# The weight-ring refills of experts with five slots or more, each issued one slot later

## The chip, the cores and the metric

The kernel runs on one core of one Trainium2 chip. The metric is the device time of one execution in microseconds (us), the median of the runs; lower is better. Engines are named as the profile names them: PE is TensorE (matmul), PEld its weight load, DVE is VectorE, ACT is ScalarE, POOL is GpSimd, SP is SyncE. SP does no arithmetic here. It issues the transfers (DMAs) one behind the other, each after the semaphore waits that it carries.

## What is computed

Attention over chunks of 64 keys, a feed-forward layer with a leaky activation, and a mixture of eight experts in which each token goes to the one expert with the largest gate value. The part that the change touches is the last:

```python
logits = x @ w_gate                       # x: 4608 tokens of 512
expert_idx = np.argmax(logits, axis=1)    # 8 experts
...
for e in range(E):
    xe = x[expert_idx == e]
    h = np.maximum(xe @ w1[e], 0.0)       # 512 -> 1024
    ye = h @ w2[e]                        # 1024 -> 512
    out[expert_idx == e] = gate_w[expert_idx == e, None] * ye
```

The reference, computed on the given inputs, sends 384, 175, 1053, 582, 1271, 128, 556 and 459 tokens to experts 0 to 7, that is 3, 2, 9, 5, 10, 1, 5 and 4 tiles of 128 tokens.

## The kernel before

The first 930 us or so hold attention, the feed-forward layer and the gate. Meanwhile the expert weights are split into two float32r parts each and written to a DRAM scratch, `wsp`, four pieces of 2 MB for each expert (two of `w1`, two of `w2`). The rest, some 440 us, runs the experts.

**Slots.** The expert part is cut into slots. A slot is one tile of up to 128 tokens of one expert. `TS` = 39 slots are unrolled in the program, and which expert a slot has is known on the chip alone: table code on DVE (the functions `table_...`) works it out from the token counts, and the slots read it from the tile `rt`. The expert with most tokens comes first, the second largest next, then the others by number, and the one with fewest slots last. With the counts above: expert 4 has slots 0 to 9, expert 2 has 10 to 18, expert 0 has 19 to 21, expert 1 has 22 and 23, expert 3 has 24 to 28, expert 6 has 29 to 33, expert 7 has 34 to 37, expert 5 has 38.

**A slot's work on PE.** `m1(t, 0)` and `m1(t, 1)` multiply the tokens by the two pieces of `w1`, `m2(t, 0)` and `m2(t, 1)` by the two pieces of `w2`, 12 matmuls each. The order on PE in the loop is m1(t+1, 0), m1(t+1, 1), m2(t, 0), m2(t, 1). All lie on line 680.

**The weight ring.** Four buffers in SBUF, `ring[0]` to `ring[3]`, hold pieces 0 and 1 of `w1` and 0 and 1 of `w2` (as buffers 2 and 3), and each has two halves: while one expert is computed from one half, the next expert's weights are loaded into the other. `refill(t, c)`, line 870, is the transfer that loads buffer c for the next expert. It is issued in every slot from 4 on, but carries a condition that SP reads from `rt` (line 866): only where the condition is 1 do its 2 MB move. In this text (t, c) is the refill of buffer c that is issued for slot t, and one whose condition is 1 is said to be sent.

**The order on SP.** The pass of the loop for slot t issues refill(t, 0), refill(t, 1), refill(t-1, 2), refill(t-1, 3), and then `load(t+4)`: four transfers of token rows (`xg`, line 648) and one of gate values (`gi`, line 651). That is nine transfers in a pass. They take turns on eight completion semaphores, and a transfer is issued once the one eight places before it is complete; a refill whose condition is 0 is complete at once. So gi waits for the first refill of its own pass, and the first, second and third refill of a pass for the second, third and fourth of the pass before. In the order list each refill also waits for the last matmuls of slot t-1 that read its buffer.

**What PE waits for.** Slots read their ring half by a register, so the program cannot tell which half a refill writes. Matmuls of slots t and t+1 are declared free of refill (t, c); those of slot t+2 on buffer c wait for it, whether it loads their half or the other one, and for a refill that is not sent that wait is nothing.

**The conditions.** `table_refill` (lines 843 to 863) writes the conditions, in rows 3 to 6 of `rt`. `mt` is the expert's number of slots less 2, `rr` the slot's place in its expert from 0, `far` is 1 for an expert of five slots or more. Only experts between the first and the last have refills (`has`).

Of the kernel before, what the change touches and what calls it, by code (L numbers as in the profile page):

```python
# [12 lines left out]
ALU = mybir.AluOpType  # L13
# [29 lines left out]
def tile_attention_moe(ctx, tc, q, k, v, w_in, w_out, alpha, w_gate, w1, w2, out):  # L43
# [15 lines left out]
    T = NTILE + 2 * (E - 1)  # L59
# [525 lines left out]
    V = nc.vector  # L585
# [134 lines left out]
    def tbl(shape, name, dt=F32):  # L720
        tb[name] = P2["tb"].tile(shape, dt, name=name)
        return tb[name]

    def bc(x, a, b, p=128):
        return x.unsqueeze(1).to_broadcast([p, b - a, E])
# [90 lines left out]
    def slot_sum(dst, vals):  # L816
        w = tb["w"][o1]
        V.tensor_tensor(out=w, in0=tb["oh"][o1], in1=vals, op=ALU.mult)
        V.tensor_reduce(out=dst, in_=w, axis=AX.X, op=ALU.add)
# [23 lines left out]
    def table_refill():  # L843
        q_ = tb["ordt"]
        mt, rr, cm, has = (tbl([1, T], x) for x in ("mt", "rr", "cm", "has"))
        mo = tbl([1, 1], "mo")
        V.tensor_reduce(out=mo, in_=tb["pos8"][o1, 1], axis=AX.X, op=ALU.max)
        V.tensor_scalar(out=has, in0=q_, scalar1=mo[:, 0:1], scalar2=None, op0=ALU.is_lt)
        V.scalar_tensor_tensor(out=has, in0=q_, scalar=0.5, in1=has, op0=ALU.is_gt, op1=ALU.mult)
        V.scalar_tensor_tensor(out=has, in0=tio[o1], scalar=tb["S"][o1, 0:1], in1=has, op0=ALU.is_lt, op1=ALU.mult)  # L850
        slot_sum(mt, bc(tb["m"][o1], 0, T, 1))
        slot_sum(rr, tb["d"][o1])
        V.tensor_copy(out=rt[:, 7, T:T + 1], in_=tb["S"][o1])
        V.tensor_scalar(out=mt, in0=mt, scalar1=-2.0, scalar2=None, op0=ALU.add)
        far = tbl([1, T], "far")
        V.tensor_scalar(out=far, in0=mt, scalar1=3.0, scalar2=None, op0=ALU.is_ge)
        for c in range(4):
            if c in (1, 2):
                V.scalar_tensor_tensor(out=cm, in0=mt, scalar=float(c - 1), in1=far, op0=ALU.min, op1=ALU.add)
                V.tensor_tensor(out=cm, in0=cm, in1=rr, op=ALU.is_equal)  # L860
            else:
                V.scalar_tensor_tensor(out=cm, in0=mt, scalar=float(c), in1=rr, op0=ALU.min, op1=ALU.is_equal)
            V.tensor_tensor(out=rt[:, 3 + c, 0:T], in0=cm, in1=has, op=ALU.mult)

    def refill(t, c):
# [23 lines left out]
    for t in range(3):  # L889
# [12 lines left out]
        (tx, 4), (m1, 3, 0), (table_order,), (m2, 1, 0), (m1, 3, 1), (m2, 1, 1), (load, 5), (m2, 2, 0), (th, 3, 0),  # L902
        (tx, 5), (m2, 2, 1), (table_next,), (load, 6), (th, 3, 1), (m1, 4, 0), (m1, 4, 1), (tx, 6), (th, 4, 0),
        (table_base, 8, T), (m2, 3, 0), (th, 4, 1), (load, 7), (m1, 5, 0), (table_refill,), (refill, 4, 0),
        (m2, 3, 1), (th, 5, 0), (m1, 5, 1), (refill, 4, 1), (load, 8), (m2, 4, 0), (th, 5, 1), (m2, 4, 1),
    )
# [125 lines left out]
```

## Time and profile before

| | |
|---|---|
| runs, median of 3 | 1383.49 us (1378.62 to 1383.83) |
| the profiled execution | 1386.75 us |
| its span, first to last instruction | 1385.0 us |
| PE busy | 1327.6 us, 96% of the span |
| DVE, ACT, POOL busy | 1029.0, 818.4, 745.7 us |

The profile is of one execution, 3.3 us above the median. Its span is read as a sequence of stages with different limits. PE is busy nearly throughout, so what counts is where it is not, and what ended those gaps. The timeline of SP shows four refills (`ring<-wsp`) in a line "x4", then four `xg` and one `gi`; it shows all refills, sent or not. The start of an issue that had to wait is the end of that wait.

### The profile page before, as it was taken

Reading aid. Unit: us, or ns where it says so; the run is one execution under the profiler, and the core shown is the slowest. Engines: PE = TensorE matmul, PEld = TensorE weight load, DVE = VectorE, ACT = ScalarE, POOL = GpSimd, SP = SyncE. Lnnn points to the kernel's source line nnn. Section 1 sums busy time; section 2 is a strip of 40 time slices with the busy share of each in tenths; the row PEclk is TensorE's granted clock in tenths of the full one; section 3 lists DMA queues with packets and bytes.
Section 4 is the critical chain, followed back from the end, with each engine's and each line's share of the span. In section 5 each row is a group of like instructions: output and inputs, shape, how many; then the busy total and the mean of one; then the engine's idle time right before and its main releaser. Section 6 shows DMA issues by size and latency. Waiting matters only on the chain. (4 is left out here: it accounts for less than half of the span.)

```text
span 1385.0 us, 31135 instructions
## 1 busy us (share of the span) xinstructions
PE 1327.6 (96%) x9515; PEld 1155.2 (83%) x9515; DVE 1029.0 (74%) x2529; ACT 818.4 (59%) x2281; POOL 745.7 (54%) x754
## 2 busy tenths in 40 slices
PE   7788999999999999999999999999999999989997
PEld 6667888999999999999989999887788888868885
DVE  7996688888788778878887886568975666546653
ACT  4554565666656565565656565439566656655663
POOL 4554456666666666666575764333444444434443
PEclk9999999999999999999999999999999999999999
DMA  6546445556556655665566561194124525866572
GB/s 233 197 151 179 145 170 191 184 190 206 200 182 191 197 190 186 206 198 168 197 200 200 182 206 39 41 370 176 47 55 157 181 66 204 331 206 229 177 273 94
DMA packets 107306, 249.16 MB, mean 180 GB/s; under 512 B 15552, under 2 KB 36544, under 8 KB 103040
## 3 DMA queue, kind: packets, MB, share of 16 engines
q1 hardware_dynamic: 101136, 227.37, 49.7%
q0 software_dynamic: 6000, 19.70, 3.7%
q8 instruction: 84, 1.38, 0.4%
q14 instruction: 86, 0.70, 0.2%
HBM read 401.39 MB, written 88.91 MB: 354 GB/s over the span
## 5 line engine op out<-in xcount | busy, mean ns | idle before, releaser
L330 PEld LDWEIGHTS h<-xt,ring 128*128 128x128 f32 x3456 | 457.0, 193 | 41.8 <-DVE xt L317 4.0
L330 PE MATMUL h<-xt,ring 128*128 128x256 f32 x3456 | 466.8, 285 | 14.3 <-DVE xt L317 3.5
L382 PE MATMUL y<-ring,g 128*128 128x512 f32 x1728 | 457.4, 400 | 5.1 <-POOL g L360 3.8
L382 PEld LDWEIGHTS y<-ring,g 128*128 128x128 f32 x1728 | 307.5, 190 | 62.7 <-POOL g L360 6.0
L360 POOL TENSOR_TENSOR g<-r,g 128x256 fp32r<-128x256 f32 x281 | 250.4, 894 | 136.9 <-ACT g L356 121.1
L406 DVE CUSTOM_DVE_ANT_0 junk<-row,wgb 128x512 bf16<-128x512 f32 x288 | 268.0, 930 | 7.8 <-ACT row L394 3.6
L470 POOL TENSOR_TENSOR sp<-eraw,sp 128x512 fp32r<-128x512 f32 x128 | 181.8, 1421 | 132.1 <-ACT sp L469 116.6
L698 DVE TENSOR_SCALAR hx<-h 32x128 f32<-32x128 f32 x576 | 165.3, 287 | 96.8 <-PE h L680 89.3
L680 PE MATMUL h<-ring,xT 128*128 (+1 forms) x936 | 221.8, 393 | 6.4 <-DMA ring<-wsp 4.4
L680 PE MATMUL y<-ring,hT 128*128 (+1 forms) x936 | 221.0, 390 | 5.8 <-POOL hT L668 3.1
L668 POOL TENSOR_TENSOR hT<-z,hT 128x512 fp32r<-128x512 f32 x78 | 101.1, 1315 | 227.6 <-ACT hT L667 227.6
L680 PEld LDWEIGHTS h<-ring,xT 128*128 128x128 f32 x936 | 177.2, 190 | 44.5 <-issue 7.0
L680 PEld LDWEIGHTS y<-ring,hT 128*128 128x128 f32 x936 | 174.9, 188 | 45.6 <-POOL hT L668 5.6
L356 ACT ACTIVATE g<-r 128x256 fp32r<-128x256 f32 x288 | 119.4, 415 | 152.0 <-DVE r L352 109.9
L346 ACT ACTIVATE r<-h 128x256 f32<-128x256 f32 x288 | 110.1, 382 | 159.3 <-POOL g L360 76.0
L696 ACT ACTIVATE hx<-h 32x128 f32<-32x128 f32 x672 | 180.3, 268 | 17.4 <-PE h L680 9.9
L667 ACT ACTIVATE hT<-z 128x512 fp32r<-128x512 f32 x78 | 48.0, 633 | 115.6 <-DVE z L665 111.3
L259 ACT ACTIVATE px<-s 32x256 f32<-32x256 f32 x240 | 89.8, 374 | 3.8 <-DVE s L248 0.9
L469 ACT ACTIVATE sp<-eraw 128x512 fp32r<-128x512 f32 x128 | 81.1, 633 | 1.0
L665 DVE STREAM_TRANSPOSE z<-xg 128x512 f32<-128x512 f32 x39 | 27.5, 706 | 47.6 <-POOL hT L668 47.6
L668 POOL TENSOR_TENSOR xT<-z,xT 128x512 fp32r<-128x512 f32 x39 | 52.1, 1336 | 16.8 <-ACT xT L667 16.3
L271 POOL TENSOR_TENSOR px<-px,sr 128x512 f32<-128x512 f32 x30 | 34.1, 1136 | 39.9 <-DVE sr L270 39.9
(737 smaller groups left out, 1193.3 us busy)
## 6 DMA issues: line engine op xcount, KB each, us to landing
ring<-wsp SPq DMA_DIRECT2D x148, 2048.0 KB
wsp<-sp SPq DMA_DIRECT2D x128, 512.0 KB
eraw<-in_w SPq DMA_DIRECT2D x128, 256.0 KB
xg<-xs SPq DMA_DIRECT2D x156, 64.0 KB
vt<-in_v SPq DMA_DIRECT2D x18, 512.0 KB
qt<-in_q SPq DMA_DIRECT2D x17, 512.0 KB
kt<-in_k SPq DMA_DIRECT2D x17, 512.0 KB
iraw<-in_w_in SPq DMA_DIRECT2D x16, 512.0 KB
```

What stands on the lines that cost most here:

```text
L259: nc.scalar.activation(out=p[J:J + 32, t], in_=s[I:I + 32, e], func=ACTF.Exp, scale=scale)
L330: nc.tensor.matmul(out=h, lhsT=w[:, wl, a, 128 * mi:128 * mi + 128], rhs=x[:, xl, a], start=(n == 0), stop=(n == 11),)
L346: nc.scalar.activation(out=r, in_=h, func=ACTF.Relu)
L356: nc.scalar.activation(out=gs[j, m][:, 0], in_=rs[j, m][0], func=ACTF.Copy)
L360: eng.tensor_tensor(out=g[:, 1], in0=r, in1=g[:, 0].bitcast(F32), op=ALU.subtract)
L382: nc.tensor.matmul(out=ys[j][t], lhsT=g[:, gl, 128 * t:128 * t + 128], rhs=w[:, wl, mi], start=(m == 0 and n == 0), stop=(m == MF - 1 and ...
L406: nc.vector.tensor_tensor_reduce(out=junk, in0=r[:, 0:512], in1=wgb[e // 2][:, e % 2], scale=1.0, scalar=0.0, op0=ALU.mult, op1=ALU.add, a ...
L470: eng.tensor_tensor(out=dst[:, 1], in0=raw, in1=dst[:, 0].bitcast(F32), op=ALU.subtract)
L668: nc.gpsimd.tensor_tensor(out=dst[:, 1], in0=z, in1=dst[:, 0].bitcast(F32), op=ALU.subtract)
L680: ins.append(nc.tensor.matmul(out=out, lhsT=lhs[:, xl, a], rhs=w[:, rows_, wl, a], start=(first and a == 0 and n == 0), stop=(last and a = ...
L696: nc.scalar.activation(out=dst, in_=src, func=ACTF.Relu)
L698: V.tensor_scalar(out=dst, in0=src, scalar1=0.0, scalar2=None, op0=ALU.max)
```

## The change

For experts of five slots or more, three of the four refills go out one slot later: buffer 0 in the second slot (before: the first), buffer 1 in the third (before: the second), buffer 2 in the fourth (before: the third). Buffer 3 stays in the fourth. For experts with fewer slots nothing changes. With the slots above the refills are sent for these slots:

| expert (slots) | buffers 0, 1, 2, 3 before | buffers 0, 1, 2, 3 now |
|---|---|---|
| 2 (10 to 18) | 10, 11, 12, 13 | 11, 12, 13, 13 |
| 0 (19 to 21) | 19, 19, 20, 20 | the same |
| 1 (22, 23) | 22, 22, 22, 22 | the same |
| 3 (24 to 28) | 24, 25, 26, 27 | 25, 26, 27, 27 |
| 6 (29 to 33) | 29, 30, 31, 32 | 30, 31, 32, 32 |
| 7 (34 to 37) | 34, 34, 35, 36 | the same |

```diff
         far = tbl([1, T], "far")
+        far2 = tbl([1, T], "far2")
         V.tensor_scalar(out=far, in0=mt, scalar1=3.0, scalar2=None, op0=ALU.is_ge)
+        V.tensor_scalar(out=far2, in0=far, scalar1=2.0, scalar2=None, op0=ALU.mult)
         for c in range(4):
-            if c in (1, 2):
-                V.scalar_tensor_tensor(out=cm, in0=mt, scalar=float(c - 1), in1=far, op0=ALU.min, op1=ALU.add)
+            if c == 0:
+                V.tensor_tensor(out=cm, in0=far, in1=rr, op=ALU.is_equal)
+            elif c < 3:
+                V.scalar_tensor_tensor(out=cm, in0=mt, scalar=float(c - 1), in1=far2, op0=ALU.min, op1=ALU.add)
                 V.tensor_tensor(out=cm, in0=cm, in1=rr, op=ALU.is_equal)
             else:
-                V.scalar_tensor_tensor(out=cm, in0=mt, scalar=float(c), in1=rr, op0=ALU.min, op1=ALU.is_equal)
+                V.scalar_tensor_tensor(out=cm, in0=mt, scalar=3.0, in1=rr, op0=ALU.min, op1=ALU.is_equal)
             V.tensor_tensor(out=rt[:, 3 + c, 0:T], in0=cm, in1=has, op=ALU.mult)
```

No instruction changes its place on PE, ACT, POOL or SP: the refills stand where they stood, and only the value that each condition has at run time differs. On DVE, in the table code between slots 4 and 5, these rows stand in another form (`cm` holds one buffer's comparison, `mt`, `rr`, `has` and `far` are as above; far_13743 is `far2`):

```order
-L856 TENSOR_SCALAR far<-mt 1x50
-L862 SCALAR_TENSOR_TENSOR cm<-mt,rr 1x50
...
-L859 SCALAR_TENSOR_TENSOR cm<-mt,far 1x50
...
+L857 TENSOR_SCALAR far<-mt 1x50
+L858 TENSOR_SCALAR far_13743<-far 1x50
+L861 TENSOR_TENSOR cm<-far,rr 1x50
...
+L863 SCALAR_TENSOR_TENSOR cm<-mt,far_13743 1x50
```

One row is added (L858), one takes another operation (L862 becomes L861), and the rows for buffers 1 and 2 read `far2` in place of `far`; nothing else on DVE moves.

## Rows read from the trace of the kernel before

**Rows 1.** The page's first line.

```profile
span 1385.0 us, 31135 instructions
```

**Rows 2.** Waits of PE, 1001 to 1366: total us, times, longest us.

```profile
PE h L680 <- DMA ring<-wsp: 4.4, 1, 4.4
PE h L680 <- DVE cm L860: 1.6, 1, 1.6
PE y L680 <- DMA ring<-wsp: 0.4, 1, 0.4
```

**Rows 3.** Timeline of PE, 1214 to 1240: start us, us, instruction, idle time before.

```profile
1217.61 2.99 PE L680 MATMUL y<-ring,hT 128*128 x12 [0.41 <-DMA ring<-wsp]
1225.01 8.17 PE L680 MATMUL h<-ring,xT 128*128 x24 [4.41 <-DMA ring<-wsp]
1233.01 5.60 PE L680 MATMUL y<-ring,hT 128*128 x24
```

**Rows 4.** Busy time, PE clock (PEclk) and DMA of three stretches, by windows.

```profile
1220.40:1225.00 4.60, 0.20 (x1) 0.02 (x1) 0.96 (x2) 2.23 (x4) 3.86 (x4) 0.83 0.59 179
1225.00:1231.00 6.00, 5.99 (x16) 4.71 (x17) 0.00 (x0) 0.45 (x2) 0.93 (x1) 0.56 0.33 88
...
1001.00:1006.00 5.00, 4.42 (x20) 3.72 (x21) 4.67 (x17) 0.83 (x2) 2.30 (x2) 1.00 0.30 93
```

**Rows 5.** The same view, 1204 to 1223; the last two columns: DMA share, GB/s.

```profile
1204.00:1223.00 19.00, 16.19 (x71) 12.82 (x69) 12.88 (x37) 10.86 (x32) 7.21 (x7) 1.00 1.01 373
```

**Rows 6.** Waits of SP's queue, 1001.5 to 1340: total us, times, longest us.

```profile
SPq L870 <- DMA ring<-wsp: 22.7, 10, 4.6
SPq L651 <- DMA ring<-wsp: 12.8, 6, 3.3
...
SPq L870 <- PE y L680: 0.2, 1, 0.2
```

**Rows 7.** Timeline of SP, 1195 to 1260 (start us, us from first to last issue).

```profile
1200.29 4.87 SPq L870 DMA_DIRECT2D ring<-wsp  x4
...
1210.72 8.11 SPq L870 DMA_DIRECT2D ring<-wsp  x4
...
1225.01 0.35 SPq L651 DMA_DIRECT2D gi<-xs  x1
1227.74 3.83 SPq L870 DMA_DIRECT2D ring<-wsp  x4
...
1237.63 3.54 SPq L870 DMA_DIRECT2D ring<-wsp  x4
...
1246.72 3.83 SPq L870 DMA_DIRECT2D ring<-wsp  x4
```

**Rows 8.** Timeline of SP, 1250 to 1385.

```profile
1280.42 3.86 SPq L870 DMA_DIRECT2D ring<-wsp  x4
...
1290.42 3.54 SPq L870 DMA_DIRECT2D ring<-wsp  x4
...
1309.38 4.46 SPq L870 DMA_DIRECT2D ring<-wsp  x4
...
1319.60 4.73 SPq L870 DMA_DIRECT2D ring<-wsp  x4
...
1334.81 34.48 SPq L870 DMA_DIRECT2D ring<-wsp  x18
```

**Rows 9.** Timeline of SP, 985 to 1200.

```profile
1055.12 4.19 SPq L870 DMA_DIRECT2D ring<-wsp  x4
...
1066.47 3.83 SPq L870 DMA_DIRECT2D ring<-wsp  x4
...
1116.90 3.55 SPq L870 DMA_DIRECT2D ring<-wsp  x4
```

**Rows 10.** Timeline of PE, 1325 to 1380.

```profile
1336.37 5.60 PE L680 MATMUL h<-ring,xT 128*128 x24
```

**Rows 11.** Timeline of DVE, 984 to 1003.

```profile
999.76 0.18 DVE L856 TENSOR_SCALAR far<-mt 1x50 f32<-1x50 f32 x1
```

## The prediction

> **What bounds the kernel now.** The first line of the page gives the span, 1385.0 us [rows 1], in an execution of 1386.75 us, so 1.75 us lie around it; that execution is 3.3 us above the median of 1383.49. I make the sum in the profiled execution's time and add the difference to the median. The change acts only on the unrolled slots, so I asked who PE waits for there [rows 2]: between 1001 and 1366 us it stands three times, 6.4 us in all. The 1.6 us at 1001 come from the table code on DVE; the other two are waits for ring transfers. The timeline of PE [rows 3] shows them. Counting 10.88 us a slot (19 blocks of 5.44 us lie between 1233.01 in rows 3 and 1336.37 in rows 10), the block at 1225.01 is m1(26), the one before it m2(24, 1). So m1(26, 0) waited 4.41 us, and what it waits for by the kernel is refill (24, 0), the first of expert 3's refills. That refill was behind others: from 1204 to 1223 the DMA engines were full (share 1.01) at 373 GB/s [rows 5], 7.1 MB, which is (22, 2), (22, 3) and (24, 0) of 2.1 MB each and the token rows. After the gap the clock was low: 0.56 of full from 1225 to 1231 [rows 4], the 1.2 GHz level for most of it, and m1(26) took 8.17 us instead of 5.60.
>
> The second view is SP's own waits [rows 6]. From 1001.5 to 1340 SP waited 35.5 us for ring transfers and 0.2 us for PE. **SP runs this stage at its own pace**: its passes are as long as their issues and the transfers that they wait for, whatever PE does. A pass that becomes late stays late, and so do all refills behind it. That decides this case.
>
> **Prices on SP**, from its timeline. A pass in which nothing is sent takes 9.1 us (1237.63 to 1246.72 [rows 7]), and its four refills go out 1.2 us apart (3.54 us for four). A pass that sends its second refill takes 9.9 to 10.0 us (1227.74 to 1237.63 [rows 7], 1280.42 to 1290.42 [rows 8]), because the next pass opens with the wait for it: from its issue (1281.6) to that point it is 8.8 us, so a lone refill is complete about 8.7 us after its issue. A pass that sends its first takes 11.35 us (1055.12 to 1066.47 [rows 9]), since its own gi waits for it. One that sends its third or fourth takes 10.2 us (1309.38 to 1319.60 [rows 8]). Two refills sent together: pass 34 sends its first two at 1319.60, and the pass behind opens at 1334.81 [rows 8], 15.2 us later, so the second is complete some 6.4 us after the first. With token rows between, the distance was 7.4 us (m2(24, 1) released at 1217.6, m1(26, 0) at 1225.0 [rows 3]). Where third and fourth were sent together, the next pass had to wait at its third refill: pass 24 needed 8.11 us for its four refills instead of 3.54 [rows 7], 4.6 us more.
>
> **Part 1, the gap goes: -7.2 us.** With (24, 0) not sent, m1(26, 0) can start behind m2(24, 1), at 1217.61 + 2.72 = 1220.33, and the block behind it at 1225.77 instead of 1233.01 [rows 3]. The shift by itself takes no time from a waiter: whoever waits for (t, c) is slot t+2, and moves with it.
>
> **Part 2, expert 2: SP late by 3.5 us.** Its refills go from passes 10, 11, 13 and 14 to passes 11, 12 and, two together, 14. One pass of 10.2 becomes one of 9.1 (-1.1); the pair costs the next pass 4.6. PE feels nothing there: the pair is sent in pass 14, near 1097 (two passes, 20 us, before 1116.90 [rows 9]), and complete near 1114.5, while m2(15, 1) comes at 1119. But SP has nothing to catch up on, since it didn't wait for PE. The added DVE row is like `far`, 0.18 us [rows 11]; it stands ahead of the conditions that SP reads, so it counts in full: with its gap 0.2 us. The other DVE rows change operation at like size, at nothing. So the passes up to 24 open 3.7 us later, and the four refills of slot 22 come as much later. (22, 1) was complete at 1200.2 (pass 23 opened on it at 1200.29 [rows 7]), 0.7 us ahead of m1(24, 1); now PE waits some 3 us there, and m2(24, 1) is released at 1221.3.
>
> **Part 3, experts 3 and 6: where PE stands at slot 36.** Pass 24's gi no longer waits (3.3 us, the longest of line 651 [rows 6]), so pass 25 opens at 1227.74 - 3.3 + 3.7 = 1228.1. It sends (25, 0), complete at 1236.8; m1(27, 0) is due at 1221.3 + 2.72 + 10.88 = 1234.9 and waits 2.0 us. Pass 26 opens at 1239.5 and sends (26, 1), complete at 1249.5, 1 us ahead of m1(28, 1). Pass 27 opens at 1249.4, pass 28 at 1258.5 and sends two together, pass 29 at 1268.7, pass 30 at 1268.7 + 9.1 + 4.6 = 1282.4. (30, 0) is complete at 1291.1, as m1(32, 0) is due (1291.3). Passes 31 to 34 open at 1293.8, 1303.7, 1312.8 and 1323.0. Pass 33 sends (32, 2) and (32, 3) together, complete at 1323.8 and 1330.2, and behind them come (34, 0) and (34, 1) of expert 7, at 1336.6 and 1343.0. Before, pass 34 opened at 1319.60 with one transfer less in front, and (34, 1) was complete at 1334.7. Now m1(36, 0), due at 1334.8, waits 1.9 us, and m1(36, 1), due at 1339.5, waits 3.6 us to 1343.1. In the trace it began at 1336.37 + 2.72 = 1339.1 [rows 10], with no ring wait behind it [rows 2]. **So PE is 4.0 us later there than before**, though the old gap is gone. What PE loses to clock or waits ahead of this point is no term of its own: the transfers set the point.
>
> **The clock after that wait.** Bounds: 0, as after the 1.6 us gap (clock 1.00 from 1001 to 1006 [rows 4]), and 2.57 us (8.17 less 5.60 [rows 3]), as after the gap of 4.41 us, of which PE was busy 0.20 in 4.60 us [rows 4]. 3.6 us is nearer to 4.41: I take 2.6.
>
> **Sum:** +4.0 + 2.6 = +6.6 us, 1393.4 in the profiled execution's time, 1390.1 at the median. Bounds: +4.0 without the clock term; +8.6 if the two last distances are 7.4 instead of 6.4 us. A difference of 0.5% (6.9 us) is about what a measurement of this kernel can tell from no change, and the forecast lies just under it.
>
> The Trainium skill (DMA: Bandwidth & Descriptors, Rules for kernel authors) says to issue a DMA early and to wait for it late; that speaks against sending a refill later. In the rows above it bears this out in part only: the waiter moves along, and what costs is the pair that the shift makes.
>
> **Rivals.** *The refills come in time.* The old gap goes and no wait takes its place: -7.2 + 0.2 = 1376.5 us. That needs (25, 0) 2 us and (34, 1) some 11 us sooner, so cheaper transfers than 8.7 and 6.4 us. Against it: both prices come from several passes. I give 0.05. The Trainium skill (DMA: Bandwidth & Descriptors, Anatomy of one DMA) has a fit, for DMAs of the other path (GpSimd's), of 2.0 us plus bytes over 436 GB/s: an estimate of 6.8 us for 2.1 MB, at which this rival would win; the trace's 8.7 us disagrees.
>
> *The lag of part 2 isn't carried*, because small slack between SP's instructions takes it up before pass 22. Then the same chain ends 3.7 us earlier: m1(36, 1) at 1339.4, +0.3 and the clock, 1383.8 to 1386.4. For it: single passes vary by about 1 us. Against it: rows 6 hold no wait for PE. 0.13.
>
> *Slower for certain: the pairs meet the token rows.* If the second of each pair comes 7.4 us behind the first, as in the gap of rows 3, passes 16 and 30 open 1 us later each, (32, 3), (34, 0) and (34, 1) lose another us each: +5, 1395 us. It decides from about 6.5 us on. 0.18.
>
> *The change doesn't reach the gap*: m1(26, 0) had waited for (22, 3) and not for (24, 0), or the slots aren't as counted. Then 1383.7 us or little more. The 7.4 us between the two releases speak against it. 0.04.
>
> **How the numbers follow.** The forecast has 0.60, 1390.1 us; some 2/5 of its own span (+4.0 to +8.6) is above +6.9, so 0.24 to slower and 0.36 to within. Slower: 0.24 + 0.18, and 0.02 of the late lag, 0.44. Within: 0.36 + 0.11 + 0.04 = 0.51. Faster: 0.05. The range goes from 1382, which takes in the lag not carried, less what the runs before differ, to 1395, the end of the slower rival.
>
> **What would show it.** Right: no ring wait at m1(26, 0); ring waits at m1(24, 1), m1(27, 0), m1(36, 0) and m1(36, 1); pass 16 opening 3 to 4 us later than 1116.90, pass 34 near 1323; third refills in passes 15, 29 and 34 waiting. Wrong: pass 16 where it was, or no ring wait behind slot 27.

## The result, and the profile after

The changed kernel takes 1392.95 us (median of 6 runs, 1391.55 to 1393.76), the kernel before 1384.15 us beside it. The ratio is 1.0069, with a 95% interval of 1.0059 to 1.0080: slower by 8 to 11 us, inside the stated range and 2.9 us above the forecast of 1390.1. It is more than the 6.9 us that the prediction took for the least that a measurement can tell; it had given 0.44 to a slowdown above that and 0.51 to a difference within it. The profiled execution has a span of 1391.7 us (before: 1385.0 [rows 1]), that is 6.7 us more. The medians differ by 2.1 us more, because the first trace of before was of an execution 2.6 us above its median and that of the changed kernel of one 0.5 us above.

The waits of PE from 1001 to 1385 us, to be read against [rows 2] (total us, times, longest us):

```profile
PE h L680 <- DMA ring<-wsp: 6.7, 4, 3.5
PE h L680 <- issue: 2.0, 1, 2.0
PE h L680 <- DVE cm L864: 1.8, 1, 1.8
```

One large wait for a ring transfer has become five smaller ones (the one put down to "issue" is one of them). The timeline of PE from 1180 to 1392, against [rows 3, 10], shows where they are:

```profile
1204.24 4.57 PE L680 MATMUL h<-ring,xT 128*128 x12 [2.03 <-issue]
...
1224.99 5.60 PE L680 MATMUL h<-ring,xT 128*128 x24
...
1236.67 5.73 PE L680 MATMUL h<-ring,xT 128*128 x24 [0.64 <-DMA ring<-wsp]
...
1292.67 5.71 PE L680 MATMUL h<-ring,xT 128*128 x24 [1.31 <-DMA ring<-wsp]
...
1339.97 4.58 PE L680 MATMUL h<-ring,xT 128*128 x12 [3.52 <-DMA ring<-wsp]
1345.77 3.01 PE L680 MATMUL h<-ring,xT 128*128 x12 [1.22 <-DMA ring<-wsp]
```

In order: m1(24, 1); m1(26), which no longer waits; m1(27, 0); m1(32, 0); m1(36, 0) and m1(36, 1). The last began at 1339.1 before and begins at 1345.8 now, 6.7 us later, which is the whole difference of the spans. Behind it both kernels run alike to the end.

The timeline of SP, against [rows 7 to 9] (start us, us from the first to the last of the pass's four refills):

```profile
1107.27 9.37 SPq L874 DMA_DIRECT2D ring<-wsp  x4
...
1122.20 3.55 SPq L874 DMA_DIRECT2D ring<-wsp  x4
...
1204.24 4.46 SPq L874 DMA_DIRECT2D ring<-wsp  x4
...
1214.28 7.63 SPq L874 DMA_DIRECT2D ring<-wsp  x4
...
1325.44 8.59 SPq L874 DMA_DIRECT2D ring<-wsp  x4
...
1345.77 30.32 SPq L874 DMA_DIRECT2D ring<-wsp  x18
```

These are passes 15, 16, 23, 24, 34 and 35 (the last line, x18, runs from pass 35 to the end). Pass 15 spends 9.37 us on four refills of which none is sent: its third waits for the second transfer of the pair that pass 14 sent. From there on SP is late: pass 16 opens at 1122.20 (before 1116.90), pass 23 at 1204.24 (1200.29). Pass 34 opens at 1325.44 (1319.60), and its own third refill waits too. m1(36, 1) begins in the very moment in which pass 35 opens, 1345.77, for both wait for refill (34, 1).

### The profile page after: what moved, and what is told of

The parts are those of the page before. It is cut to its first block, busy times and chain, and to the rows that moved or that the text cites. A ratio compares the mean times of both kernels' runs of the same rounds, so it can differ in the third digit from the quotient of the medians.

```text
span 1391.7 us, 31136 instructions
## 1 busy us (share of the span) xinstructions
PE 1332.3 (96%) x9515; PEld 1158.5 (83%) x9515; DVE 1029.3 (74%) x2530; ACT 817.5 (59%) x2281; POOL 745.8 (54%) x754
## 5 line engine op out<-in xcount | busy, mean ns | idle before, releaser
L680 PE MATMUL h<-ring,xT 128*128 (+1 forms) x936 | 224.7, 396 | 10.5 <-DMA ring<-wsp 6.7
```

Source lines behind the costliest of these rows:

```text
L680: ins.append(nc.tensor.matmul(out=out, lhsT=lhs[:, xl, a], rhs=w[:, rows_, wl, a], start=(first and a == 0 and n == 0), stop=(last and a = ...
```

## The experiments

Each is compared with the kernel before on the same chip; times are ratios of the runs, and us at 1384 us for the ratio. On that footing the change itself costs 9.5 us (1.0069), by the medians 8.8. The diffs of the first five kernels are against the changed kernel, that of the last is against the kernel before.

**The moves without the pair, and the pair without the moves.** The change does two things to an expert of five slots or more: it sends buffers 0 and 1 a slot later, and it puts buffer 2 beside buffer 3. The first kernel does the one alone:

```diff
             if c == 0:
                 V.tensor_tensor(out=cm, in0=far, in1=rr, op=ALU.is_equal)
-            elif c < 3:
-                V.scalar_tensor_tensor(out=cm, in0=mt, scalar=float(c - 1), in1=far2, op0=ALU.min, op1=ALU.add)
+            elif c == 1:
+                V.scalar_tensor_tensor(out=cm, in0=far, scalar=2.0, in1=rr, op0=ALU.mult, op1=ALU.is_equal)
+            elif c == 2:
+                V.scalar_tensor_tensor(out=cm, in0=mt, scalar=1.0, in1=far, op0=ALU.min, op1=ALU.add)
                 V.tensor_tensor(out=cm, in0=cm, in1=rr, op=ALU.is_equal)
```

> Buffers 0 and 1 are moved as in the change, buffer 2 stays in the third slot as before, so no two refills go out together for an expert of five slots or more (it also needs one DVE row less than before). Theory (the moved first refill takes the old gap away, and the pair of third and fourth refills that the change makes is what costs): SP opens pass 16 within 1 us of 1116.9, no ring wait at slots 24 and 36, a ring wait of about 2 us at m1(27, 0) and no other; 5 us faster than before (4 to 7), near 1379. Rival (what costs is that each moved refill comes a slot nearer to its readers): the ring waits at slots 32 and 36 stay, and the time is that of the changed kernel less 2 us at most, 1390 to 1393.

Measured: 0.9987 (0.9972 to 1.0002, 12 runs), 1.8 us faster, with no change still inside the interval; the profiled execution took 1380.72 us. Its ring waits of PE from 1001 to 1385, and passes 15 and 16 of SP:

```profile
PE h L680 <- DMA ring<-wsp: 1.2, 1, 1.2
...
PE y L680 <- DMA ring<-wsp: 0.2, 1, 0.2
```

```profile
1107.61 3.54 SPq L874 DMA_DIRECT2D ring<-wsp  x4
...
1116.70 3.55 SPq L874 DMA_DIRECT2D ring<-wsp  x4
```

In this trace the places are as the theory says: no wait in pass 15, pass 16 at 1116.70, and of ring waits that at m1(27, 0), 1.2 us, beside one of 0.2 us at m2(24, 1). The rival is out, being 8 us off. But the size was expected at 5 us (4 to 7) and is under 4, so that part of the forecast failed; two more traces, below, go after the reason.

The second kernel moves buffer 2 alone, with buffers 0 and 1 as before:

```diff
             if c == 0:
-                V.tensor_tensor(out=cm, in0=far, in1=rr, op=ALU.is_equal)
-            elif c < 3:
-                V.scalar_tensor_tensor(out=cm, in0=mt, scalar=float(c - 1), in1=far2, op0=ALU.min, op1=ALU.add)
+                V.scalar_tensor_tensor(out=cm, in0=mt, scalar=0.0, in1=rr, op0=ALU.min, op1=ALU.is_equal)
+            elif c == 1:
+                V.tensor_tensor(out=cm, in0=far, in1=rr, op=ALU.is_equal)
+            elif c == 2:
+                V.scalar_tensor_tensor(out=cm, in0=mt, scalar=1.0, in1=far2, op0=ALU.min, op1=ALU.add)
                 V.tensor_tensor(out=cm, in0=cm, in1=rr, op=ALU.is_equal)
```

> Only buffer 2 is moved: buffers 0 and 1 go out in the first and second slot as before, buffers 2 and 3 together in the fourth. Theory: the old gap at m1(26, 0) stays, and the pairs make SP late as in the change: pass 15 takes about 5 us more for its four refills, ring waits at m1(24, 1), m1(26, 0), m1(36, 0) and m1(36, 1); about 11 us slower than before (8 to 13), so slower than the changed kernel. Rival (the shift of buffers 0 and 1 costs, not the pair): within 2 us of before.

Measured: 1.0065 (1.0046 to 1.0084), 9 us slower. The timeline of PE, 1190 to 1392:

```profile
1203.86 2.99 PE L680 MATMUL h<-ring,xT 128*128 x12 [1.73 <-DMA ring<-wsp]
...
1227.92 7.12 PE L680 MATMUL h<-ring,xT 128*128 x24 [4.45 <-DMA ring<-wsp]
...
1342.08 4.19 PE L680 MATMUL h<-ring,xT 128*128 x12 [3.28 <-DMA ring<-wsp]
1347.88 3.00 PE L680 MATMUL h<-ring,xT 128*128 x12 [1.62 <-DMA ring<-wsp]
```

The waits are at m1(24, 1), m1(26, 0), and slot 36, as expected; the rival (within 2 us) is out. The pair alone costs what the whole change costs. This kernel keeps the old gap of 4.45 us and the low clock behind it (7.12 us for the block), and by the ratios it is no slower than the changed one, which has neither (1.0065 and 1.0069, the intervals cover each other). I had expected it 2 us slower than that, and the traces show this much: its m1(36, 1) begins 2.1 us later than that of the changed kernel (1347.88 against 1345.77), its span is 1.3 us longer. So beside the pair, the gap of 7.2 us that the change removes is worth little, nothing by the ratios and some 2 us by the traces: the rest of what PE gains at slot 26 it waits for at slot 36.

**The nine-slot expert apart from those of five.** Here the change is made for the two experts of five slots alone, and for the expert of nine alone, by masking the shift (`sh`, and `fs` in place of `far2`; `is_lt` becomes `is_ge` in the other kernel):

```diff
+        V.scalar_tensor_tensor(out=sh, in0=mt, scalar=6.5, in1=far, op0=ALU.is_lt, op1=ALU.mult)
+        V.tensor_tensor(out=fs, in0=far, in1=sh, op=ALU.add)
...
+            if c < 2:
+                V.tensor_tensor(out=cm, in0=(sh, fs)[c], in1=rr, op=ALU.is_equal)
```

> The change for the two experts of five slots alone; the expert of nine slots sends its refills as before (same number of DVE rows as the changed kernel). Theory (SP's lag from the nine-slot expert's pair is carried to slot 22 and on): pass 16 opens near 1117, no ring wait at m1(24, 1), still one at m1(27, 0) and those at slot 36; 2 us slower than before (0 to 4). Rival (that lag is taken up before it counts): the time of the changed kernel, 8 to 9 us slower than before.

> The change for the nine-slot expert alone; the two experts of five slots send as before. Theory: pass 16 opens near 1122 and the lag is carried: ring waits at m1(24, 1) and, as before but later, at m1(26, 0); 3 to 5 us slower than before, though neither the pair nor any transfer of that expert makes PE wait in its own slots. Rival (lag taken up): as before within 1 us.

Measured: the five-slot experts alone 1.0029 (1.0017 to 1.0041), 4 us slower; the nine-slot expert alone 1.0035 (1.0024 to 1.0046), 4.8 us slower. Together that is 8.8 us, about the cost of the change (8.8 to 9.5). PE of the first, 1190 to 1392, has no wait at m1(24, 1) and those of slots 27, 32 and 36:

```profile
1231.64 5.70 PE L680 MATMUL h<-ring,xT 128*128 x24 [0.54 <-DMA ring<-wsp]
1287.49 5.68 PE L680 MATMUL h<-ring,xT 128*128 x24 [1.19 <-DMA ring<-wsp]
1334.44 4.20 PE L680 MATMUL h<-ring,xT 128*128 x12 [3.19 <-DMA ring<-wsp]
1340.32 2.96 PE L680 MATMUL h<-ring,xT 128*128 x12 [1.68 <-DMA ring<-wsp]
```

PE of the second, in the same stretch, has the wait at m1(24, 1) and the old gap, 1.3 us later than before, and none at slot 36; its SP shows the wait in pass 15:

```profile
1202.19 3.00 PE L680 MATMUL h<-ring,xT 128*128 x12 [1.11 <-DMA ring<-wsp]
1226.30 7.28 PE L680 MATMUL h<-ring,xT 128*128 x24 [4.42 <-DMA ring<-wsp]
```

```profile
1104.57 9.20 SPq L876 DMA_DIRECT2D ring<-wsp  x4
...
1119.32 3.55 SPq L876 DMA_DIRECT2D ring<-wsp  x4
```

Pass 16 was expected near 1122 and opens at 1119.32, but this execution is early: pass 15 opens 3.2 us sooner than before (1107.81), and from pass 15 to 16 it takes 14.75 us, before 9.09. So a pair that makes no one wait in its own expert (slots 10 to 18) costs 4.8 us a hundred microseconds later. Some 0.5 us of either time can be the table code, which has two rows more ahead of the first condition (from the start of `far` to the end of the first row of `rt` 1.00 us, before 0.53). Both rivals are out. The four us of the first kernel are at the edge of what was expected (0 to 4).

**A smaller transfer.** The changed kernel, in which buffer 2's refills from slot 24 on are half as large (they leave out the second float32r part of the piece):

```diff
+        part = slice(0, 1) if c == 2 and t >= 24 else slice(0, 2)
         dma = nc.sync.dma_start(
-            out=W2[c][:, bass.ds(dh, 1)].bitcast(F32),
-            in_=wsp[bass.ds(nx, 1), c].bitcast(F32).rearrange("e p h k f -> p e h k f"),
+            out=W2[c][:, bass.ds(dh, 1), part].bitcast(F32),
+            in_=wsp[bass.ds(nx, 1), c, :, part].bitcast(F32).rearrange("e p h k f -> p e h k f"),
```

> The changed kernel, in which the refills of buffer 2 that are issued for slots 24 and later move only the first of the two float32r parts, 1 MB in place of 2 (the second part in the ring stays that of an earlier expert, so this part of the computation is left wrong). The number and the slots of the refills are those of the change. Theory (the end is set by the chain of SP's passes and the transfers in front of refill (34, 1)): the fourth refill of each pair is complete 3 us sooner, pass 29's wait and pass 34's shrink by as much, pass 30 opens 3 us sooner than in the changed kernel, and the waits of 3.5 and 1.2 us at slot 36 are gone but for 1 us; 4 to 6 us faster than the changed kernel, so 3 to 5 us slower than before. Rival (the time is lost at slots 24 to 28, with the nearer refills and the low clock): within 1.5 us of the changed kernel.

Measured: 1.0030 (1.0012 to 1.0048), 4.2 us slower than before, some 5 us less than the change costs, as the theory has it. PE, 1001 to 1385, and passes 34 and 35 of SP:

```profile
PE h L680 <- DMA ring<-wsp: 4.1, 2, 2.1
```

```profile
1319.56 5.86 SPq L875 DMA_DIRECT2D ring<-wsp  x4
...
1337.76 30.31 SPq L875 DMA_DIRECT2D ring<-wsp  x18
```

The two waits left are at m1(24, 1) (2.12 us) and m1(27, 0) (1.98 us), ahead of any smaller transfer. Pass 34 opens 5.9 us and pass 35 8.0 us sooner than in the changed kernel (1.3 us of either lie ahead of slot 24, by the start of m1(24, 1), 1202.95 against 1204.24), and slot 36 has no wait. The number and the slots of the refills are those of the change, so it is the transfers' length in front of (34, 1) and in SP's chain that set the end, and not that refills go out nearer to their readers.

**Why the kernel without the pair gains so little.** It was traced twice more, and the kernel of before once more:

> The kernel without the pair once more, unchanged, for a second trace: its first trace had ring waits of 1.4 us in all and a span 6.0 us under that of before, while its median is only 1.9 us under. Theory (executions differ in how late the transfers of slot 22 come, and this kernel has under 1 us of room at slots 24 to 28): a slower execution shows larger ring waits at m1(24, 1), m2(24, 1) or m1(27, 0), with a low clock behind them. Rival (the executions differ ahead of the slots): slot 6 starts later than at 1002 and the waits are as in the first trace.

> The kernel without the pair a third time, for a third trace; the same two theories as for its second.

> The kernel of before once more, for a second trace, since the first was of an execution 2.7 us above the median of its 27 runs. Theory: the gap at m1(26, 0) is there again, of 3 to 5 us, and the low clock behind it varies with it; where the time is under 1385 the low stretch is shorter. Rival: the gap is much smaller in most executions, so that there was less to gain than 7.2 us.

They took 1382.45, 1381.03 and 1385.31 us. PE from 1190 to 1392 in the second and the third trace of the kernel without the pair:

```profile
1229.50 5.71 PE L680 MATMUL h<-ring,xT 128*128 x24 [0.47 <-DMA ring<-wsp]
1329.35 2.98 PE L680 MATMUL h<-ring,xT 128*128 x12 [1.59 <-DMA ring<-wsp]
1334.85 4.58 PE L680 MATMUL h<-ring,xT 128*128 x12 [2.51 <-DMA ring<-wsp]
```

```profile
1229.81 5.75 PE L680 MATMUL h<-ring,xT 128*128 x24 [0.30 <-DMA ring<-wsp]
1333.86 2.98 PE L680 MATMUL h<-ring,xT 128*128 x12 [3.05 <-DMA ring<-wsp]
```

Neither theory was right: the waits that grew are not at slots 24 to 27. They are at slot 36 again, at the readers of (34, 0) and (34, 1). In the two traces m1(36, 1) begins as pass 35 opens, that is as (34, 1) is complete:

```profile
1334.84 31.90 SPq L874 DMA_DIRECT2D ring<-wsp  x18
```

```profile
1333.85 30.29 SPq L874 DMA_DIRECT2D ring<-wsp  x18
```

In the kernel before, (34, 1) was complete some 4.4 us ahead of its reader (1334.7 against 1339.1). With the gap at slot 26 gone PE comes to slot 36 up to 8.6 us sooner (due at 1327.8 in the second trace, 1336.37 before), so this room is used up, and more can be had only if (34, 1) comes sooner too. In the first trace it did (pass 35 opened at 1331.97), and nothing waited at slot 36. The second trace of before has the gap once more:

```profile
1223.86 7.94 PE L680 MATMUL h<-ring,xT 128*128 x24 [4.30 <-DMA ring<-wsp]
```

Gap and block are within 0.3 us of those of the first, so the rival of a smaller gap finds nothing in its favour; this execution isn't under 1385 us, so whether faster ones have a shorter low stretch stays open. Slot 36 explains why less than 7.2 us is gained; it doesn't by itself explain a gain as small as 1.8 us. The three spans are 2.8 to 6.0 us under the two of before, and none of the three traces is of an execution near the upper end of that kernel's runs (1385.25 us).

**A version that beats both.** If slot 36's refills are the next bound, then (34, 0) and (34, 1) mustn't stand behind each other in one pass. Buffer 1 is sent in buffer 2's slot for all experts, which moves it for those of three and four slots too, from slots 19 and 34 to 20 and 35:

```diff
         for c in range(4):
-            if c in (1, 2):
-                V.scalar_tensor_tensor(out=cm, in0=mt, scalar=float(c - 1), in1=far, op0=ALU.min, op1=ALU.add)
+            if c == 0:
+                V.tensor_tensor(out=cm, in0=far, in1=rr, op=ALU.is_equal)
+            elif c == 1:
+                V.scalar_tensor_tensor(out=cm, in0=mt, scalar=1.0, in1=far, op0=ALU.min, op1=ALU.add)
                 V.tensor_tensor(out=cm, in0=cm, in1=rr, op=ALU.is_equal)
-            else:
-                V.scalar_tensor_tensor(out=cm, in0=mt, scalar=float(c), in1=rr, op0=ALU.min, op1=ALU.is_equal)
+            elif c == 3:
+                V.scalar_tensor_tensor(out=cm, in0=mt, scalar=3.0, in1=rr, op0=ALU.min, op1=ALU.is_equal)
             V.tensor_tensor(out=rt[:, 3 + c, 0:T], in0=cm, in1=has, op=ALU.mult)
```

> The kernel without the pair, and in addition buffer 1 goes out in the same slot as buffer 2 for every expert, so also for the experts of three and four slots one slot later than before: slots 20 and 35 in place of 19 and 34 (buffer 2's refill of a slot is issued a pass later than buffer 1's, so this makes no pair). Theory (what bounds the kernel without the pair is SP's chain at slots 24 to 28 and the two refills (34, 0) and (34, 1) behind each other at slot 36): SP opens pass 23 some 3 us sooner than 1200.3, no ring wait is left behind 1002 us, and the 4.4 us between (34, 1) and its reader no longer limit; 6 us faster than before (4 to 7.5). Rival (the kernel without the pair is bound by something else, so that a further gap removed brings nothing): its time, 2 us faster than before.

> The same kernel once more, for a second trace: by the theory no ring wait either, or one under 1 us.

Measured: 1376.91 us, 0.9954 (0.9936 to 0.9972), 6.4 us faster than before; the second trace is of an execution of 1379.95 us. The ring waits of PE from 1001 to 1385 in the first trace, where the one wait is, and passes 19, 20, 34 and 35 of its SP:

```profile
PE h L680 <- DMA ring<-wsp: 0.4, 1, 0.4
```

```profile
1229.33 5.72 PE L680 MATMUL h<-ring,xT 128*128 x24 [0.36 <-DMA ring<-wsp]
```

```profile
1143.32 3.85 SPq L872 DMA_DIRECT2D ring<-wsp  x4
...
1154.80 3.85 SPq L872 DMA_DIRECT2D ring<-wsp  x4
...
1315.40 4.90 SPq L872 DMA_DIRECT2D ring<-wsp  x4
...
1329.01 32.79 SPq L872 DMA_DIRECT2D ring<-wsp  x18
```

Passes 19 and 20 before, against these:

```profile
1145.21 4.12 SPq L870 DMA_DIRECT2D ring<-wsp  x4
...
1159.65 3.80 SPq L870 DMA_DIRECT2D ring<-wsp  x4
```

Where the pairs are gone the passes are shorter: pass 19 takes 11.48 us (before 14.44), pass 34 takes 13.61 us (before 15.21 [rows 8]). In the second trace these are 11.82 and 12.24 us. One ring wait of 0.36 us is left behind slot 6, at m1(27, 0); the second trace has none there. The rival (2 us faster) is out. The 6.4 us come near the 7.2 us that the old gap and its low clock had cost in the trace of before. Two pairs were taken apart at once, at slots 19 and 34, and no run tells how much each gave.

## Why the prediction was right, step by step

**The direction and the bound.** That SP runs the slots at its own pace, so that a pass that becomes late stays late, was the reason to forecast a slower kernel although the gap goes. The runs bear it out: the change for the nine-slot expert alone, whose pair makes nobody wait in its own slots, costs 4.8 us.

**Part 1, the gap of 7.2 us** was right and worth little here. m1(26) has no wait and a full clock after the change, but the kernel that keeps the gap and has the pair is as fast by its ratio, and 2 us later at slot 36 by its trace.

**Part 2, SP's lag.** The wait of the pass behind a pair was put at 4.6 us, from pass 24 of before; pass 15 had 5.8 (9.37 less 3.54). So pass 16 opened 5.3 us late and not 3.7. Some of it was made good in passes 21 and 22: pass 23 was 3.95 us late, and pass 24, at 1214.28, 3.56 us. There the forecast (3.7) fits. The wait at m1(24, 1), forecast as 3 us, was 2.03, since PE came 1.3 us later: m1(24, 0) began at 1199.33 (before 1198.00), after a loss at slot 6 for which the prediction had no term on PE (last section).

**Part 3, the chain to slot 36.** Pass 25 opened at 1227.48 (forecast 1228.1), pass 30 at 1283.37 (1282.4), pass 33 at 1315.76 (1312.8), pass 34 at 1325.44 (1323.0):

```profile
1227.48 3.82 SPq L874 DMA_DIRECT2D ring<-wsp  x4
```

```profile
1283.37 3.86 SPq L874 DMA_DIRECT2D ring<-wsp  x4
...
1315.76 4.09 SPq L874 DMA_DIRECT2D ring<-wsp  x4
```

Up to pass 30 the working holds to 1 us; passes 30 and 31 took 0.7 us more than their prices in all, and pass 32 took 10.4 us instead of 9.1. m1(27, 0) waited 0.64 us (forecast 2.0), since PE came 1.1 us later; m1(32, 0) waited 1.31 (forecast none). At slot 36 both readers waited, as forecast, though the longer wait came first; m1(36, 1) began 6.7 us later than before and not 4.0. This is the term that was mis-sized: 2.4 us of it is the opening of pass 34.

**The clock term** is the step that failed. 2.6 us were added for a low clock behind the wait for (34, 1). The waits at slot 36 were 3.5 us and then 1.2, and not 1.9 and then 3.6, so the low clock fell on m1(36, 0), between them. The clock of PE in the stretches before, in and behind that block (the last three columns: PE clock, DMA share, GB/s):

```profile
1336.40:1339.90 3.50, 0.06 (x1) 0.00 (x0) 1.50 (x3) 2.42 (x4) 2.51 (x2) 1.00 1.02 433
1339.90:1344.60 4.70, 4.58 (x12) 3.36 (x12) 0.00 (x0) 0.12 (x1) 2.31 (x2) 0.64 0.98 332
1344.60:1348.00 3.40, 2.23 (x10) 1.91 (x11) 0.00 (x0) 3.21 (x13) 0.00 (x0) 1.00 0.12 42
```

The block took 4.58 us instead of some 2.9, and that was hidden, because m1(36, 1) had to wait for (34, 1) anyway. Behind it the clock was full and 12 matmuls took 3.01 us. So the clock cost nothing, and the sum of +6.6 came out near the +6.7 of the traces by luck: two misses, of 2.7 and 2.6 us, cancel.

**The rivals.** The refills come in time: they don't, there are five waits. The lag isn't carried: it is, by the run of the nine-slot expert, though not in full (5.3 us at pass 16, 3.6 us at pass 24). The pairs meet the token rows: m1(36, 0) and m1(36, 1), released by two refills of one pass, lie 5.8 us apart, so at slot 36 the distance within a pair wasn't longer than the 6.4 us of the sum; at pass 15 the wait behind a pair was, by 1.2 us, but by pass 24 that was made good. Of the 2.4 us at pass 34, pass 27 (10.86 us instead of 9.1) and pass 32 bring more than all. The change doesn't reach the gap: it does.

**What stays open.** The medians differ by 8.8 us, the two traces by 6.7, and both traces of before (1386.75 and 1385.31 us) show the same gap and waits. Where an execution of before of 1380 us differs from them wasn't seen, and so the small gain of the kernel without the pair (1.8 us) stays without a full reason.

## What to carry to other kernels

Where an engine issues transfers in a line, with waits on earlier ones of the same line, its passes are a chain of their own: work out when each pass opens before asking what a moved transfer does, since a wait put into the line delays all that is issued behind it. A gap on the bounding engine is worth only the room that the next reader has (here 4.4 us at slot 36 before, not 7.2, unless its transfer comes sooner too), so look for that room before making the gap smaller. Spread transfers over the passes: sending buffers 0 and 1 later gave 1.8 us with the pairs of experts 0 and 7 left, and 6.4 us with those taken apart as well. Pairs are still there in that kernel: expert 0 sends its last two refills in one pass, and expert 1 all four in two.

## What the hardware showed that was not expected

The length of a gap on PE alone doesn't tell whether the clock falls. In the changed kernel 1.82 us at slot 6 were enough, where 1.60 us before had left it full [rows 2, 4]; the block took 7.34 us instead of 5.71. The first line is of before, the second of the changed kernel, and the third is the changed kernel's clock (third column from the end), 0.68 of full, a mean of the low level (1.2 GHz) and the full one:

```profile
1001.58 5.71 PE L680 MATMUL h<-ring,xT 128*128 x24 [1.60 <-DVE cm L860]
```

```profile
1001.75 7.34 PE L680 MATMUL h<-ring,xT 128*128 x24 [1.82 <-DVE cm L864]
```

```profile
1001.00:1006.00 5.00, 4.25 (x12) 3.50 (x13) 4.67 (x17) 0.80 (x2) 2.28 (x2) 0.68 0.24 80
```

At this one place the twelve traces part cleanly: seven gaps of 1.60 to 1.73 us left the clock full (5.70 to 5.73 us for the block), five of 1.81 to 2.08 us did not (7.31 to 7.34 us). Elsewhere they don't. The 2.03 us at m1(24, 1) of the changed kernel were followed by 4.57 us for 12 matmuls, but 2.12 us at the same place in the kernel with the smaller transfers by 2.99 us, and 3.05 us at slot 36 in the third trace of the kernel without the pair by 2.98 us, a full clock (1.00 by the trace).

The added DVE row of 0.2 us thus cost PE 1.8 us at slot 6. It cost the kernel next to nothing: m1(24, 1) waits 2.03 us for a transfer that SP's chain sets, and would have waited that much longer.
